# PSUM banks with two accumulators accessed in two rounds, the tail rows of the weight sums stored interleaved, and a new instruction order

## The chip, the core and the metric

The kernel runs on one core of a Trainium2 chip (TensorE, VectorE, ScalarE, GpSimd, the sync engine SP, and 16 DMA engines that all queues share). The metric is device time of one execution in microseconds. In the profile TensorE is PE (matmuls) and PEld (weight loads), VectorE is DVE, ScalarE is ACT and GpSimd is POOL.

## What is computed

Three blocks follow each other, each on the whole output of the one before. A recurrence over 768 tokens for 4x8 heads of width 40, a mixing block with two Fourier transforms and a channel MLP, and a mixing block with a token MLP and a channel MLP:

```python
for t in range(S):                                   # attention
    y[:, :, t] = einsum('bhd,bhde->bhe', rt, state)
    Sa = einsum('bhde,bhe->bhd', state, at)
    state = state * wt[:, :, None, :] - einsum('bhd,bhe->bhde', Sa, bt) + einsum('bhd,bhe->bhde', vt, kt)
...
u = x + real(fft(fft(x, axis=1), axis=2))            # block 1, x is 4 x 768 x 320
ch = relu(norm(u) @ w_ch1) @ w_ch2                   # 320 -> 1280 -> 320
x = u + ch
...
u = x + (relu(x.T @ w_tok1) @ w_tok2).T              # block 2, over tokens
out = u + relu(u @ w_ch1) @ w_ch2                    # 320 -> 1536 -> 320
```

The weights arrive as 64-bit floats; the kernel decodes them on the chip into a high and a low 32-bit part, and a product is three matmuls (high by high, high by low, low by high).

## The kernel before, in words

**Stages.** The recurrence runs in 12 chunks of 64 tokens. Then come block 1's channel MLP in six groups of 512 tokens, with the Fourier transforms of the next batch between them; the token MLP; and block 2's channel MLP, again in six groups. TensorE does all products, ScalarE and VectorE read PSUM (ScalarE makes the high part, VectorE subtracts it to get the low part), GpSimd adds.

**What sets the order.** The code makes a list of 4654 operations with costs and dependencies (class `Plan`). The string `ORDER`, found beforehand by a planner, says in which order they are written into the program; each engine then runs its own instructions in that order and none overtakes another. The keys that an operation reads and writes (lists `R` and `W` of `P.op`) are what the planner knows of its dependencies. The waits that are built into the program are not made from those keys: the tile framework makes them from the tiles, and takes a whole PSUM tile, here one bank, as one thing, in the order in which its accesses are written. A token `+m,bank,j` puts in m filler matmuls (`warm`, L54).

**The weight sums (`vset`).** Block 2's first channel weight is used in a scheme with seven products in place of eight (below), which needs sums of its quarters. While block 1's channel MLP runs on TensorE, VectorE and GpSimd decode four quarters, GpSimd forms the sums, and each of the seven matrices is split into a high part (tile `mdh`, three buffers, written by ScalarE at L838) and a low part, which go to a table `vS` in memory. There are four such sets: two column halves, each with 128-row parts (`part==0`, stored at L841) and with the 64 tail rows (`part==1`, stored at L842). A set makes 14 stores, on the SP queue:

```python
if part==0: ... nc.sync.dma_start(out=o(y),in_=fl(v()))
else: ... nc.sync.dma_start(out=o(2).rearrange("(a b p) n -> b a p n",a=2,b=2)[y],in_=fl(v())[0:64])
```

The tail's target has 2 blocks (a) of 32 rows (p) of 384 numbers; the source is 64 partitions. ScalarE can fill an `mdh` buffer again only when the store out of it has landed, and VectorE the buffers `mda`, `mdt` and `mdraw` likewise. Behind such a waiting instruction on ScalarE and VectorE stand the channel MLP's own instructions: `ch1` (L1049, tile `hps`, 8 matmuls of 512 columns) is followed by ACT L1051 and DVE L1052 (tile `cc`, high and low part), and `ch2` (L1039, tile `acc`, 12 matmuls of 320 columns) needs both.

**Another store for comparison.** `dr_T<-Y` (L992) has a target of 4 blocks of 32 rows: `s.Td[j][q].rearrange("p i x -> i p x")`, with i=4 first.

**The seven products (`ch7`, `ch1`).** A unit (36 of them: six groups by six) makes seven products of four matmuls of 256 columns (L1086), called 0 to 6 here. It has two banks, `sa` and `sb`, each with two accumulators of 256 columns: R0 and R1 in `sa`, R2 and R3 in `sb`. Product 0 goes to R0, 1 to R1, 2 to R2, 3 to R3; then 4 is added on to R0, 5 to R2 and 6 to R3. Between these the accumulators are read: ACT copies R0 (L1096) and R2 (L1099) after products 0 and 2, DVE adds R1 and R3 to earlier sums (L1093) after products 1 and 3. At the end R0 is read by the two relu steps (ACT L1091, DVE L1092), and R2 and R3 by DVE adds. Odd units use another pair of banks than even ones, so unit u+2 takes over the banks of unit u. `ch2` (L1075) is 12 matmuls of 320 columns into `acc`, twice a unit.

Of the kernel before, what the change touches and what calls it, by code (L numbers as in the profile page):

```python
# [540 lines left out]
34 85:1 32 35 86 36 83 37 88:1 38 8b:0 3a 89 8y 8e:1 8c 39 8f 3b 94 8k 3c 8l 93 3d 3e 92 3g 8m +7,y,0 95:0 3f 3h 9h:1 96 3i 9e:0 9i 3j 8o 3m 9b:1 9f
3n 8q 3k 98:0 9c 8p 3q ce:1 99 e6 8n e4 9k:1 cg kt 3l 8j cf 87 c1 84 8a 9l 3o 9p 9o 3p 3s c0 dx 8d e0 c2 9n e1 3t 8g e2 mv 97 3r 9g 3u 3x e5 hr 3v 3w
hx 9t e3 9q hs hw e7 ba ht e8 f3 e9 f2 hy b9 hu +12,y,0 ea:0 my bb 9r eb 9u bd 9v 9w +2,y,0 ej:1 ez 9x 9y 9z 9s a0 a1 bc a2 a3 +2,y,0 ed:0 fo a4 a5
be:2 qp ee a6 bf 48 bg a7 ek bh aa bi a8 +2,y,0 ep:0 em:1 a9 eq bj ab ca +3,y,0 bk:0 ae hp ac +1,y,0 bl bm af eg:0 ad bn eh ag f4:1 f5 ah en f6 aj bo
es +1,y,0 f7 ai el et bp mz ak 9a f9 +2,y,0 ck:2 al f8 an 9j am cl +2,y,0 ch:0 er ao cm ap cj ar ci 49 +2,y,0 cz:1 ev hv cs:1 d0 eu 4a cn:2 ct ef i0
fa:0 cv ey cu fb co cx:0 cw cq ew fc aq cy cp ex i1 d4:0 as cr f1 av fd d5 d1:1 f0 at 4b aw fe dc:0 fn az ff g1:1 d7 b0 dd d6 au hz g4:2 ax g3 9d d2
ib:0 g2 ay de ol g6 b3 i2:1 mw ic b1 g5 i8:0 i3 b4 ei df b2 ie:1 i9 id b5 b8 d9:0 i4 4c d3:0 4d d8 4e da 4i ga:0 if b7 eo db gb g7:1 4f b6 gc gn:1 4g
g9 4h ih:0 gp i5:1 k9 go k8 gi:2 4j ii 4k g8 k6 dg i6 4m gd:0 4n im ik gj ij di:0 il gl gk gq ge dl:1 ia gt:0 gg dm fp gr:1 9m fr dj i7 kb:1 dh dn fs
do gh +2,m,1 kc gu kd fq ke gm in gs gf +2,t,0 dk:0 ku 4l dp kf 4o kn:0 dq kg dr 4p dv ft:1 ko h6:0 ds fu ig kp:0 dt ec h7 fv:1 du kq gy:1 h8 fw ny h9
l8:2 gz ir ka is it iu ip gv:0 iv la iw l9 fx:0 k7 ix iy kr:1 h1 fy iz kv lb:0 gw ks j0 o2 j1 fz:0 ld tu h3:1 n0 lc kh:1 mx g0 ki io +1,y,0 kj h0 h4  # L550
n1 kk iq n2 o3:2 kl gx:0 j2 h2 km j3 h5 n6 j4 j5 ha n7 j7 lh:0 n8 hb hc:0 li hf:1 hd lj kw j6 hg +1,t,0 he:0 kx hh j8 hi le:1 kz jb hj lf j9 of:1 lg
on jc o4 og o5 vw jd o6 o0 oh:0 n3 o7 ly:1 jg o8 nc:0 ja oi lz hk oj:0 je n9:1 hl ok qr jf ky qq l0:1 jh lk:0 o1 n4 l1 hm lu:0 jk hn n5 m0:1 lp:1 4s
# [755 lines left out]
```

## Time and profile before

| | |
|---|---|
| median of 3 runs | 1048.67 us (1048.01 to 1056.04) |
| the profiled execution's own time | 1046.91 us |
| its span, first to last instruction | 1044.9 us |
| PE busy in the span | 942.1 us (90%) |
| DVE, ACT, POOL busy | 702.3, 492.2, 370.9 us |
| mean granted TensorE clock | 0.962 |

PE is the engine that is busy nearly always, but a busy PE is not a PE at its peak. So the stretches in which it is idle, or at a lower clock, and what ended each wait, are to be looked for. A mean over the whole span hides that the stages differ: some have almost no gap, two have many.

### The profile page before, as it was taken

How to read it: one execution, taken by the hardware profiler on the slowest of the kernel's cores; microseconds unless marked ns; L12 is line 12 of the kernel's file. 1: busy time of each engine (PE TensorE's matmuls, PEld its weight loads, DVE VectorE, ACT ScalarE, POOL GpSimd, SP SyncE). 2: the span in 40 equal slices, each digit the busy share in tenths (PEclk: the TensorE clock that was granted, in tenths of full speed). 3: DMA queues.
4: the chain of work that ended last, by engine and by line, in shares of the span. 5: the costliest groups of instructions: out<-in, count | busy, mean ns of one | idle time of the engine just before them, and what ended most of it. 6: DMA issues, size and time to landing. Idle time of an engine off the chain costs nothing.

```text
span 1044.9 us, 24118 instructions
## 1 busy us (share of the span) xinstructions
PE 942.1 (90%) x9621; PEld 857.4 (82%) x9621; DVE 702.3 (67%) x1543; ACT 492.2 (47%) x1068; POOL 370.9 (35%) x504
## 2 busy tenths in 40 slices
PE   7569999999999989999979869999998998998997
PEld 5558888888888888889858758999898888998887
DVE  8799598979687479996837235626767474654544
...
GB/s 219 182 153 144 188 192 192 180 206 193 174 161 204 269 273 249 210 150 101 127 88 160 41 88 89 127 334 219 153 86 83 64 41 41 85 47 21 1 33 25
DMA packets 153446, 146.13 MB, mean 140 GB/s; under 512 B 101303, under 2 KB 126967, under 8 KB 152567
## 3 DMA queue, kind: packets, MB, share of 16 engines
...
q14 instruction: 36, 0.29, 0.1%
...
## 4 chain that ended last, share of the span: by engine, by line
PE 32%; DVE 6%; DMA 6%; ACT 2%; POOL 2%; issue 2%; SPq 1%; DVEq 0%; ACTq 0%; POOLq 0%
PE acc L1075 10%; PE sb L1086 5%; PE hps L1049 5%; PE acc L1039 4%; PE sa L1086 4%; DMA dr_vS<-mdh 3%; PE tps L1182 2%; DVE W1t L1092 2%; DMA dr_vS<-mdraw 1%; DVE C L1093 1%; PE t2ps L1195 1%; DMA dr_vS<-mda 1%; DVE cc L1004 1%; ACT W1t L1091 1%; POOL C L1101 1%
## 5 line engine op out<-in xcount | busy, mean ns | idle before, releaser
L1039 PE MATMUL acc<-W,cc 128*128 128x320 f32 x720 | 123.4, 321 | 23.1 <-DVE cc L1052 17.2
L1039 PEld LDWEIGHTS acc<-W,cc 128*128 128x128 f32 x720 | 113.2, 195 | 31.2 <-DVE cc L1052 19.8
L1049 PE MATMUL hps<-cc,W1t 128*128 128x512 f32 x480 | 123.8, 403 | 1.0 <-DVE cc L1025 0.9
L1049 PEld LDWEIGHTS hps<-cc,W1t 128*128 128x128 f32 x480 | 90.4, 194 | 18.9 <-DVE cc L1025 1.4
L1101 POOL TENSOR_TENSOR C<-C,C 128x256 f32<-128x256 f32 x36 | 27.7, 770 | 209.4 <-DVE W1t L1092 105.8
L1093 DVE TENSOR_TENSOR C<-sb,C 128x256 f32<-128x256 f32 x108 | 44.9, 422 | 52.0 <-PE sb L1086 47.2
L1051 ACT ACTIVATE cc<-hps 128x512 fp32r<-128x512 f32 x60 | 35.5, 595 | 89.9 <-PE hps L1049 89.9
L54 PE MATMUL warm<-ident 128*128 128x128 f32 x450 | 74.2, 305 | 3.6 <-POOL ident masks.py:199 2.0
L1092 DVE SCALAR_TENSOR_TENSOR W1t<-C,W1t 128x256 fp32r<-128x256 f32 x108 | 46.1, 439 | 43.6 <-ACT W1t L1091 43.2
L1052 DVE SCALAR_TENSOR_TENSOR cc<-hps,cc 128x512 fp32r<-128x512 f32 x60 | 41.2, 687 | 50.2 <-ACT cc L1051 49.8
L226 POOL TENSOR_SCALAR_AFFINE_SELECT RT<-RT 64x384 f32<-64x384 f32 (+1 forms) x72 | 44.8, 643 | 78.3 <-ACT RT L136 73.9
L1075 PE MATMUL acc<-v,W1t 128*128 128x320 f32 x432 | 70.3, 314 | 2.4 <-DVE W1t L1092 1.0
L1091 ACT ACTIVATE W1t<-C 128x256 fp32r<-128x256 f32 x108 | 42.5, 414 | 63.3 <-DVE C L1093 60.5
L1075 PE MATMUL acc<-vb,W1t 128*128 128x320 f32 x432 | 68.7, 310 | 2.9 <-DVE W1t L1092 2.9
L216 PE MATMUL kg<-am,bt 120*128 120x192 f32 x242 | 55.8, 366 | 16.7 <-ACT am L136 13.2
L54 PEld LDWEIGHTS warm<-ident 128*128 128x128 f32 x450 | 65.1, 213 | 5.9 <-POOL ident masks.py:199 2.0
L417 POOL TENSOR_SCALAR_AFFINE_SELECT sc<-sc 64x384 f32<-64x384 f32 (+1 forms) x72 | 40.7, 565 | 80.9 <-ACT sc L136 78.8
L1075 PEld LDWEIGHTS acc<-v,W1t 128*128 128x128 f32 x432 | 65.1, 192 | 3.7 <-DVE W1t L1092 1.7
L1075 PEld LDWEIGHTS acc<-vb,W1t 128*128 128x128 f32 x432 | 63.7, 188 | 4.1 <-DVE W1t L1092 3.9
L216 PEld LDWEIGHTS kg<-am,bt 120*128 120x128 f32 x242 | 42.6, 208 | 21.8 <-ACT am L136 14.2
L407 PE MATMUL sc<-rm,VZd 120*128 120x192 f32 x264 | 58.7, 354 | 1.7 <-issue 1.1
L859 POOL TENSOR_TENSOR mda<-mda,mdh 128x320 f32<-128x320 f32 (+2 forms) x32 | 29.7, 934 | 82.9 <-ACT mdh L856 54.9
...
## 6 DMA issues: line engine op xcount, KB each, us to landing
...
```

The costliest lines, as they stand in the source:

```text
L54: for x in range(m): nc.tensor.matmul(t[:,128*(x%4):128*(x%4)+128],lhsT=ident,rhs=ident,start=True,stop=True)
L216: nc.tensor.matmul(ps[:,192*x:192*x+192],lhsT=bt[:,g+x].rearrange("p v t -> p (v t)"),rhs=am[:,:,g+x],start=True,stop=True)
L226: nc.gpsimd.affine_select(out=kv,in_=kv,pattern=[[0,3*m],[1,L]],compare_op=ALU.is_gt,fill=0.0,base=0,channel_multiplier=-1)
L407: for x,g in enumerate(gs): nc.tensor.matmul(ps[:,192*x:192*x+192],lhsT=VZd[:,g].rearrange("p v t -> p (v t)"),rhs=s.rm[:,:,g],start=True, ...
L1039: nc.tensor.matmul(s.pst(acc[x]),lhsT=a[:,sl],rhs=w2(w,m),start=(m==0 and n==0),stop=(m==MT-1 and n==2))
L1049: for n,(l,r) in enumerate(ops): nc.tensor.matmul(ps,lhsT=l,rhs=r,start=n==0,stop=n==7)
L1052: s.dve(.61,lambda: nc.vector.scalar_tensor_tensor(out=t["hl"][z],in0=s.pst(h),scalar=0.0,in1=t["hh"][z].bitcast(F32),op0=ALU.max,op1=ALU. ...
L1075: nc.tensor.matmul(s.pst(acc[x]),lhsT=a[:,sl],rhs=wv(w),start=(u==0 and y==0 and k==0),stop=(u==5 and y==1 and k==2))
L1086: for n,(y,x) in enumerate(((0,0),(0,1),(1,0),(2,2))): nc.tensor.matmul(R[r](),lhsT=va(q,y),rhs=S[:,x],start=first and n==0,stop=last and ...
L1091: s.act(256,lambda: nc.scalar.activation(out=Hh(y,c),in_=src(),func=AF.Relu),rd,[('Hh',z,y,c)],free=free)
L1092: s.dve(.33,lambda: V.scalar_tensor_tensor(out=Hl(y,c),in0=src(),scalar=0.0,in1=Hh(y,c).bitcast(F32),op0=ALU.max,op1=ALU.subtract),rd+[('H ...
L1093: def add(n,r,m,free): s.dve(.33,lambda: V.tensor_tensor(out=C(n),in0=R[r](),in1=C(m),op=ALU.add),[K[r],('C',m)],[('C',n)],free=free)
```

## The change

Four things are changed. The keys of the accumulators become the banks themselves: the planner now takes two accumulators of a bank as one thing. The code of a unit is written so that accesses to a bank alternate in two rounds: both first products, both reads, the later product or products, the last reads. The tail rows' target is walked with p first and a second, and the host lays out the weight's tail rows so that each comes twice in a row (row 2p+a is tail row p for both a), which leaves the contents of `vS` as they were. The estimate of that store's cost is .00097 for .00095 per column. `ORDER` is a new string for all 4654 operations, with 235 filler matmuls where there were 225.

```diff
 ORDER="""
-0 1 5 4 7 8 2 6 3 9 1e 1g 1i a 3y 1h 7q 1f 40 41 e 44 42 3z f g 43 45 b c h 7o +12,y,0 c3:0 fm j bx c4 i bq:1 8t k c5:0 br l m bs:1 1j o n 46 1k d 47
+0 1 5 4 7 8 2 6 9 3 1e 1g a 1i 3y 1h 1f 7q 40 41 44 e 42 3z f g 43 45 b c j h 7o +12,y,0 c3:0 fm i bq:1 c4 bx k c5:0 8t l br m 1j bs:1 o n 46 1k d 47
...
@@ vset
-                else: P.op('SP',.5,lambda y=y,v=v,o=o: nc.sync.dma_start(out=o(2).rearrange("(a b p) n -> b a p n",a=2,b=2)[y],in_=fl(v())[0:64]),kv,[('mv',c,q,2+y)],due=due,data=d*.00095)
+                else: P.op('SP',.5,lambda y=y,v=v,o=o: nc.sync.dma_start(out=o(2).rearrange("(a b p) n -> b p a n",a=2,b=2)[y],in_=fl(v())[0:64]),kv,[('mv',c,q,2+y)],due=due,data=d*.00097)
@@ ch7, ch1
-            K=[pa+(0,),pa+(1,),pb+(0,),pb+(1,)]
+            K=[pa,pa,pb,pb]
...
-            x0=prod(0,0,True,False,[ha[0],hb[0]])
-            s.act(256,lambda: nc.scalar.activation(out=C(p1),in_=R[0](),func=AF.Copy),[K[0]],[('C',p1)],free=fa)
-            prod(1,1,False,True,after=[x0]); add(u2,1,p1,fa)
-            x2=prod(2,2,True,False,after=[x0])
-            s.act(256,lambda: nc.scalar.activation(out=C(p5),in_=R[2](),func=AF.Copy),[K[2]],[('C',p5)],free=fb)
-            prod(3,3,False,False,after=[x2]); add(u3,3,u2,fb)
+            x0=prod(0,0,True,False,[ha[0],hb[0]]); prod(1,1,False,True)
+            s.act(256,lambda: nc.scalar.activation(out=C(p1),in_=R[0](),func=AF.Copy),[K[0]],[('C',p1)],free=fa); add(u2,1,p1,fa)
+            prod(2,2,True,False,after=[x0]); prod(3,3,False,False)
+            s.act(256,lambda: nc.scalar.activation(out=C(p5),in_=R[2](),func=AF.Copy),[K[2]],[('C',p5)],free=fb); add(u3,3,u2,fb)
...
-            prod(5,2,False,True); add(c12,2,u2,fb); relu(0,1,lambda: C(c12),[('C',c12)])
-            prod(6,3,False,True); add(c21,3,u2,fb); relu(1,0,lambda: C(c21),[('C',c21)])
+            prod(5,2,False,True); prod(6,3,False,True)
+            add(c12,2,u2,fb); relu(0,1,lambda: C(c12),[('C',c12)])
+            add(c21,3,u2,fb); relu(1,0,lambda: C(c21),[('C',c21)])
@@ kernel (host layout)
-            f = [np.arange(128), 128 + np.arange(128), np.tile(np.arange(256, 288), 4), np.tile(np.arange(288, 320), 4)]
+            f = [np.arange(128), 128 + np.arange(128), np.tile(np.repeat(np.arange(256, 288), 2), 2), np.tile(np.repeat(np.arange(288, 320), 2), 2)]
```

**Place 1, SP queue, the last set of tail stores (second column half).** Before (L842 is the tail store, L825 and L852 are loads of weights; the numbers behind the shape name the semaphores waited for):

```order
L825 DMA mdraw0_4881<-in_moe2_w_ch1_dram 128x768 [waits DMAHW4_49]
L842 DMA dr_vS_183<-mdh0_4884 2x32x384 [waits DMAHW5_49,Activation_49]
L842 DMA dr_vS_183<-mdh0_4884 2x32x384 [waits Activation_49]
L842 DMA dr_vS_183<-mdh1_4888 2x32x384 [waits DMAHW7_49]
L842 DMA dr_vS_183<-mdt1_4886 2x32x384 [waits DMAHW0_49,Pool_49]
```

And now (the tail store is L843, the loads L826 and L853):

```order
L842 DMA dr_vS_183<-mdh1_4888 128x384 [waits DMAHW4_49]
L843 DMA dr_vS_183<-mdh1_4888 32x2x384 [waits Activation_49]
L843 DMA dr_vS_183<-mdh0_4884 32x2x384 [waits DMAHW6_49,Activation_49]
L843 DMA dr_vS_183<-mda2_4891 32x2x384 [waits DMAHW7_49,Pool_49]
L843 DMA dr_vS_183<-mdh0_4884 32x2x384 [waits DMAHW0_49,Activation_49]
```

The stores stay 14 a set, in another sequence; their target's first dimension is 32 where it was 2.

**Place 2, PE in the first group of the seven-product stage, just behind the second block of `acc` matmuls.** Before, two units alternate (banks `sa_8889` and `sb_8894` are one unit's, `sb_8820` the unit before it):

```order
L1086 MATMUL sa_8889<-cc_5535,vc_8273 128x256 [waits DMASW3_49]
L1086 MATMUL sa_8889<-cc_5535,vc_8273 128x256 x3
L1086 MATMUL sb_8894<-cc_5535,vc_8273 128x256 [waits DMASW2_49,DVE_49]
L1086 MATMUL sb_8894<-cc_5535,vc_8273 128x256 x3
L1086 MATMUL sa_8889<-cc_5535,vc_8273 128x256 x4
L1086 MATMUL sb_8894<-cc_5535,vc_8273 128x256 x4
L1086 MATMUL sb_8820<-cc_5535,va_8138 128x256 [waits DVE_49]
L1086 MATMUL sb_8820<-cc_5535,va_8138 128x256 x3
L1086 MATMUL sb_8820<-cc_5535,va_8138 128x256 [waits Activation_49]
L1086 MATMUL sb_8820<-cc_5535,va_8138 128x256 x3
```

And now (`sa_8900` and `sb_8915` are one unit's, `sa_8828` and `sb_8833` the unit before it):

```order
L1087 MATMUL sa_8900<-cc_5555,vc_8286 128x256 [waits DMASW3_49,DVE_49]
L1087 MATMUL sa_8900<-cc_5555,vc_8286 128x256 x7
L1087 MATMUL sa_8828<-cc_5555,va_8190 128x256 [waits DVE_49,Activation_49]
L1087 MATMUL sa_8828<-cc_5555,va_8190 128x256 x3
L1087 MATMUL sb_8915<-cc_5555,vc_8286 128x256 [waits DMASW2_49]
L1087 MATMUL sb_8915<-cc_5555,vc_8286 128x256 x3
L1087 MATMUL sb_8833<-cc_5555,va_8190 128x256 [waits DVE_49,Activation_49]
L1087 MATMUL sb_8833<-cc_5555,va_8190 128x256 x7
L1087 MATMUL sb_8915<-cc_5555,vc_8286 128x256 x4
```

Products 0 and 1 stand together (x1 and x7), and 5 and 6 of the earlier unit stand together behind one wait, where they were two steps with a wait each.

**Place 3, DVE in the second group.** Before, the two last reads of bank `sb_9143` stand apart (C is a sum, L1092 the low part of a relu, L988 and L989 transposes for a later group):

```order
L1093 TENSOR_TENSOR C5_8741<-sb_9143,C1_8737 128x256 [waits DVE_49,PE_49]
L1092 SCALAR_TENSOR_TENSOR W1t_5548<-sa_9134,W1t_5548 128x256 [waits Activation_49]
L989 STREAM_TRANSPOSE Y_5534<-X_4867 128x4x32 [waits DMAHW6_49,DMAHW7_49,DMAHW5_49,DMAHW4_49]
L988 STREAM_TRANSPOSE Y_5534<-X_4867 128x2x4x32
L989 STREAM_TRANSPOSE Y_5534<-X_4867 128x4x32 x3
L988 STREAM_TRANSPOSE Y_5534<-X_4867 128x2x4x32 x2
L989 STREAM_TRANSPOSE Y_5534<-X_4867 128x4x32 x2
L1093 TENSOR_TENSOR C4_8740<-sb_9143,C1_8737 128x256
L1092 SCALAR_TENSOR_TENSOR W1t_5548<-C4_8740,W1t_5548 128x256 [waits Activation_49]
L1093 TENSOR_TENSOR C1_8737<-sa_9217,C0_8736 128x256 [waits PE_49]
```

And now (the adds are L1094, the low part L1093):

```order
L1094 TENSOR_TENSOR C5_8747<-sb_9154,C1_8743 128x256 [waits DVE_49,PE_49]
L1094 TENSOR_TENSOR C4_8746<-sb_9154,C1_8743 128x256 [waits DVE_49]
L1094 TENSOR_TENSOR C1_8743<-sa_9228,C0_8742 128x256 [waits DVE_49,Activation_49]
L1094 TENSOR_TENSOR C3_8745<-sb_9237,C1_8743 128x256 [waits DVE_49,Activation_49]
L1093 SCALAR_TENSOR_TENSOR W1t_5568<-C4_8746,W1t_5568 128x256 [waits Activation_49]
```

Both last reads of a bank stand together, and so do the next unit's two adds.

## Rows read from the trace of the kernel before

**Rows 1.** The page's first line.

```profile
span 1044.9 us, 24118 instructions
```

**Rows 2.** Busy time by stretch: us; busy (instructions) of PE, PEld, DVE, ACT, POOL; PEclk, DMA share, GB/s.

```profile
520.00:625.00 105.00, 81.83 (x402) 70.87 (x401) 46.95 (x110) 29.02 (x64) 36.82 (x37) 0.89 0.29 95
625.00:703.00 78.00, 78.00 (x445) 70.45 (x444) 38.14 (x74) 22.78 (x45) 29.09 (x37) 1.00 0.59 173
758.00:1045.00 287.00, 258.54 (x1834) 246.08 (x1834) 162.09 (x422) 92.78 (x269) 57.53 (x76) 0.99 0.14 47
```

**Rows 3.** Waits, 500 to 625 us: total us, times, longest.

```profile
ACT mdh L838 <- DMA dr_vS<-mdh: 26.4, 8, 7.1
PE acc L1039 <- DVE cc L1052: 16.4, 6, 8.7
...
DVE mda L855 <- DMA dr_vS<-mda: 9.5, 2, 7.6
...
PE acc L1039 <- ACT cc L1051: 5.8, 4, 3.7
```

**Rows 4.** DVE's timeline, 600 to 620 us: start, us, instruction, idle before it.

```profile
610.48 0.49 DVE L855 SCALAR_TENSOR_TENSOR mda<-mdraw,mdt 128x320 int32<-128x320 int32 x1 [7.56 <-DMA dr_vS<-mda]
...
611.50 0.68 DVE L1052 SCALAR_TENSOR_TENSOR cc<-hps,cc 128x512 fp32r<-128x512 f32 x1
```

**Rows 5.** Busy time by stretch: tail stores alone, `dr_T` stores alone, 128-row stores.

```profile
602.00:611.00 9.00, 1.51 (x8) 1.03 (x6) 1.37 (x4) 0.47 (x1) 0.00 (x0) 0.77 0.13 50
865.00:869.00 4.00, 3.26 (x25) 2.84 (x23) 0.17 (x1) 0.97 (x3) 0.00 (x0) 1.00 0.26 102
...
497.00:499.00 2.00, 2.00 (x15) 1.81 (x15) 1.93 (x4) 1.09 (x2) 1.47 (x2) 1.00 1.02 368
```

**Rows 6.** The chain that ended last, 584 to 618 us: start, us, what.

```profile
579.89 4.27 DMA dr_vS<-mdh
...
587.33 10.44 DMA dr_vS<-mdh
...
601.35 10.96 DMA dr_vS<-mdraw
```

**Rows 7.** PE's timeline, 505 to 640 us.

```profile
527.29 1.73 PE L1039 MATMUL acc<-W,cc 128*128 128x320 f32 x10 [1.49 <-DVE cc L1052]
528.86 2.02 PE L1049 MATMUL hps<-cc,W1t 128*128 128x512 f32 x8
...
535.95 3.04 PE L1039 MATMUL acc<-W,cc 128*128 128x320 f32 x10 [4.23 <-DVE cc L1052]
...
612.24 3.04 PE L1039 MATMUL acc<-W,cc 128*128 128x320 f32 x10 [8.72 <-DVE cc L1052]
...
622.73 2.56 PE L1049 MATMUL hps<-cc,W1t 128*128 128x512 f32 x8
```

**Rows 8.** Waits of the weight loads, 757 to 1045 us: total us, times, longest.

```profile
PEld sb L1086 <- ACT C L1099: 9.2, 16, 1.5
PEld sb L1086 <- DVE C L1093: 7.9, 9, 1.6
PEld sa L1086 <- ACT C L1096: 7.6, 12, 1.4
PEld acc L1075 <- DVE W1t L1092: 5.7, 7, 1.6
PEld sb L1086 <- DVE W1t L1092: 3.1, 4, 1.6
```

**Rows 9.** The chain, 760 to 766 us.

```profile
762.00 1.43 PE sb L1086 x12
763.43 1.76 PE acc L1075 x12
```

**Rows 10.** Groups by shape, 700 to 1045 us: busy us, mean ns, idle before and releasers.

```profile
L1093 DVE TENSOR_TENSOR C<-sa,C 128x256 f32<-128x256 f32 x36 | 15.2, 423 | 13.3 <-PE sa L1086 7.3 <-ACT W1t L1091 2.3 <-issue 2.2
...
L1096 ACT ACTIVATE C<-sa 128x256 f32<-128x256 f32 x36 | 13.7, 381 | 67.1 <-PE sa L1086 57.8 <-DVE C L1093 6.2 <-issue 2.9
```

More of the change, by code (lines that the diff above doesn't have):

```diff
@@ L541 @@
[L541 to L552, printed above, removed]
@@ new lines @@
+1mj +6,t,0 1lw:0 1mp 1m1 1mk 1mr 1mh 1mx:0 1mt 1ms 1oq 1m2 1n6 1ov 1oy 245 1mw:2 1mv:1 1p8 246 1oz 1p9 1p0 1mu 1n7 1p5 1pb +10,t,0 1n2 247 1my 1n8 248
+1n9 1n3 24d 1mz 1p1 1m3 1ot 1n4 1qb 1n0 1n5 1qi 1na +10,t,0 1nf:2 1qd 24a 1n1 1ng 249 +1,y,0 1nb:0 1pc 24g 1nh 1ou 1q1 1nc 1ni 24i 1nd 1qf 24e 1ow 1pi
+24b 1ne 24j 1pa 1qc +7,acc,0 22z:0 299 234:1 24f 24c 1pd 232 230 235 1pe 231 +2,acc,0 239:0 237 1qe 233 1p2 1pg 23d:1 1pf 236 1pr 238 24o:0 1pj 1qk
+23c 250:1 1qh 1q2 23a 1pl 23b 24h 23e 298 23f 1pm 23g 1qn 1q3 23h 251 29g 24p 1p3 23i 252 23j 253 24q 1p4 254 24r +12,acc,0 24k:1 23k 1qg 1p6 23l
@@ new lines @@
+25v 1rl 1rk 1s2 25t 1rp 1rn 264 1rm 1s3 25w:1 1sb 1rs 1s4 1ro 25u 1rt 1rq 1rv 1ru 1s9 25z 29m 25x 1rz 1rw 1s5 1sl 1rx 276:0 1sc 1s6 1ry 1sv 1sd 1s0
+277 1s7 25y 1se 1sf +2,ps,0 26a:1 1sm 1sg 1s8 278 279 1sn 1sa 1sj 1sh 26d 1t5 26b 265:0 1sp 1sw 1sq 27a:1 1si 266 268 267 1sx 1sk 26e:0 27b 1sz 269
+1t6 27c 29r:1 26c 29n:0 26f 1sy 1t7 27d 26g 1t0 29o 1so 26h 1t9 26i 29s 1st 1sr 29p 27e 1t8 26j 26k 1td 29q 1tb 26l 1tr 26m 1tf 2a3:0 26n 1t1 29t 26o
+29u 26v 27h 26t 1ta 26x:1 2cp 1tl 29v:1 26y 26w 26u 270:0 1tc 26z 29w 271 29x +1,acc,3 273:1 1t2 27f 1te 29y 274 272 +2,acc,3 29z:1 1ss 1t4 275 1t3
@@ new lines @@
+27i 1su +1,acc,1 27j:0 27g 2co 28h 1tg 2cq 27m:1 27k 1th 27l 1tm 27p:3102 1ti 27n 2cr 28k 1tn 2cs 2cx 27o 27q:0 1ts 28j 1tt 2cy 27t 27r 1tj 2cz 1to
+1u0 28e 1tp 27u:1 1tu 1tq 27s 28f 27x 2ct 27v 2cu 28i 1tv 28g 28l 2a4 27y:0 2d0 2cv 1tw 2a5 27w 1tk 1u7 281 2a0 1u9 27z 1u1 1vb 1tx 2a1 280 282:1 1tz
+1ty 28m:0 285 1u8 28n 1uf 28o 1ua 283 1u2 1ub 286:0 1uj 1ud 1u3 284 1uk 1uh 2a2 1ul 28p:1 1u4 1um 287 289 28q 1u5 1uz 288 1u6 28a:0 2cw 1ug 28r 28d
+1uc 1ui 1ur 28b 1us 1ue 1un 28c 28v:1 1uo 1uu 1vc 1uq 1vd 28y 1up 28w 2a6 1ve 1v5 1uv 1vf 28z:0 1v0 1uw 28x 2a7 1v1 1uy 28s:1 290 1v2 292 28t 1v3 291
@@ new lines @@
+22o 2it 2iu 2iz 2j0:1 2ix 2iy 2j3 2j4:0 2j1 2j2 2j7 22w 22y 2f6 2fe 2fl 2fj 2fg 2fi 2f7 2fc 2f9 2fh 2f8 2fa 2ff 2fb 2fd 2fk 2j5 2jd 2jn 2jl 2jj 2jp
+2je 2jm 2jr 2jt 2j6 2j8 2jk 2jo 2jv:1 2jz:0 2ju 2jq 2js 2jw 2k0 2jf 2jg 2ji 2jh 2jc 2jb 2k7 2k8 2k3 2k4 2k5 2k6 2jx 2jy 2kf:1 2k1 2k2 2kr:0 2ks
++2,acc,1 2kp:0 2kd 2ke 2k9 2ka 2kb 2kc 2kg 2kh 2l6 2l5 2kq 2kt:0 2l4 2l2 2l3 2l7 2ki 2ku 2la 2l8 2l9 2kn:1 2ko 2kz 2l1 2l0 2lc 2le 2ld 2ja 2kj:0 2md
+2me 2mh 2kk 2kl 2mi 2mn 2mo 2j9 2km 2kx:1 2ky 2kv:0 2kw 2ml 2n1:1 2n2 2n5:0 2n6 2mj 2mk 2n3:1 2n4 2mf 2mg 2mp:0 2mt:1 2mm 2mq 2mu 2nb 2nc 2nd 2ne 2mr
```

219 lines of the change are left out of this document (108 added, 111 removed).

## The prediction

> **What bounds the kernel now.** I read the profile in this order: the page's head, the busy time by stretch, the waits of the stretches with gaps, and then the timelines and the chain at the longest waits.
>
> The span is 1044.9 us [rows 1]; the profiled execution took 1046.91 us, so 2.0 us lie around the span, and it stands 1.8 us under the median of 1048.67. The sum below is made against 1044.9 + 2.0. By stretch [rows 2], PE has two kinds of life. From 625 to 703 us it is busy 78.00 of 78.00 us at granted clock 1.00; nothing can be won there. From 520 to 625 it is busy 81.83 of 105 at clock 0.89, so 23.2 us are idle and some of the busy time is slow. From 758 to 1045 it is busy 258.54 of 287 at clock 0.99, so 28.5 us are idle in many small pieces (at the weight loads, which come just ahead of the matmuls, a little more is idle). The change touches just these two stretches. In both, DVE, ACT and POOL are busy less than 57% [rows 2]: they don't lack time, they wait in line.
>
> *500 to 625.* PE waits 16.4 us in 6 waits for DVE's `cc`, and 5.8 in 4 for ACT's, 22.2 in all, while ACT waits 26.4 us for stores out of `mdh` to land, and DVE 9.5 out of `mda` [rows 3]. The link is the in-order queue: at 610.48 DVE's L855 has sat 7.56 us on a store out of `mda`, and the `cc` instruction that PE wants starts only behind it, at 611.50 [rows 4]. PE's `acc` row at 612.24 then shows 8.72 us of idle ended by that `cc` [rows 7]. Why do the stores land late? While tail stores run alone, the DMA share is 0.13 and 50 GB/s flow: two engines' worth of sixteen. A transfer with 4 as its target's first dimension has 0.26 and 102 GB/s, and the 128-row stores of the same set 1.02 and 368 GB/s [rows 5]. A tail store is 2x32x384x4 B = 98,304 B, so 1.97 us at 50 GB/s; one that finds nothing ahead lands in 4.27 us, those behind others in 10.44 and 10.96 [rows 6]. Then the clock: after the idle times seven of PE's rows are slow, from the one at 535.95 (3.04 us, where the same `acc` row takes 1.73) to the one at 622.73 (2.56 against 2.02) [rows 7]. A 3.04 us row is one largely at 1.2 GHz in place of 2.4. The seven excesses sum to 8.4 us. This stretch so loses 22.2 + 8.4 = 30.6 us.
>
> *758 to 1045.* The weight loads wait for reads of the banks `sa` and `sb` by ACT's copies and DVE's adds: 9.2 + 7.9 + 7.6 = 24.7 us in 37 waits of at most 1.6 us; the next two, 5.7 and 3.1 us, are for the low part of relu, that is for a reader at a unit's end [rows 8].
>
> **The change part by part.**
>
> *Tail stores.* They stay 28 of 96 KB, their target becomes 32x2x384. The bytes are the same. Rows show 2 first for two engines, 4 first for four, 128 first for all [rows 5]; 32 first is not among them. Nearest to 32 are the two ends 4 and 128: between 102 and 368 GB/s, a store takes between 0.96 and 0.27 us, and 28 of them 27 or 7.5 us where 55 are spent now. I take the 128 end, because the share doubled when the first dimension did, and 32 gives each of 16 engines two rows. The Trainium skill ("DMA: Bandwidth & Descriptors", section "Why a DMA increments its semaphore by 16 and not by 1") has a rule: the number of engines is the largest one up to 16 that divides the slowest dimension of both sides. By it the old store had 2 engines, which agrees with 0.13 [rows 5], and the new one has 16; that it is 16 for 32 no run here shows yet. By the rule the part gains the 26 us worked out below; by the row with 4 it gains some 15.
>
> What is won: with landings near the fixed part (4.27 - 1.97 = 2.3 us, plus 0.3 to 1.0) rather than 10 us, three `mdh` buffers are enough for ACT, and the 22.2 us of PE's idle time and the 8.4 us of slow clock that follows it have no cause left. What is late next is the chain of a set itself: load, DVE, POOL's sums, ACT's high part, DVE's low part, store. Its engines are busy 46.95, 29.02 and 36.82 of 105 us [rows 2], so it fits beside some 24 us of PE work per set, but not without a wait where ACT refills a buffer whose store has just gone. I leave 1.15 us for each of four sets, 4.6 in all. **Gain 26 us**, at most 30.6. At the least 15: if the four-engine price held and half of the waits stayed (11.1) with half of the slow clock (4.2). On the SP queue stores and loads only change places (14 stores a set before and now); a load behind a store's wait is issued earlier when that wait is shorter. The host's doubled tail rows are no work on the chip.
>
> *Two rounds per bank.* The waits that are built in take a bank as one thing, in the order of the writing. Before, product 1 went to R1 beside R0, and the add of R1 or a later product stood behind accesses that it has no need of: in the written order 20 of the 36 adds of R1 stand behind product 4, though only R0 is touched by that. What decides whether PE waits is the distance from a write to the next write of the same bank, counted in PE's own work: a product is 1.43/3 = 0.48 us, an `acc` row 1.76 [rows 9]. Counted so through the order of before, product 1 to 4 is 2.0 us on average, 13 of 36 under 1.2; product 3 to 5 is 3.1; 5 to 6 is 3.1 with six under 1. Through the order of now: 1 to 4 is 6.0 (least 1.8), 3 to 5 is 6.4 (one of 0.5, the next 2.2), and 5 and 6 stand together. Between the writes one ACT copy (0.381 us) and one DVE add (0.423) [rows 10] have to be done, 0.8 us back to back; with what lies between them I put 1.3, an estimate from the longest waits of 1.4 to 1.6 [rows 8]. Before, many distances were shorter than that or were so with one other instruction ahead in the reader's queue; now only one is. So nearly all of the 24.7 us lose their cause: I take 22.
>
> What it costs: a bank is held longer. The next unit but one gets `sa` 5.2 us after the last write (9.2 before), `sb` after 4.5 (4.8); 34 handovers each. Before, `sb` at 4.8 cost 3.1 us in 4 waits [rows 8]; `sa` at 5.2 should then cost nearly the same, and I take 2 us more than now. The stage's products and `acc` rows are the same 252 of the one and 72 of the other. **Gain 20 us**; at least 8 (a third of the 24.7 goes, as it would if the queues of ACT and DVE and not the distances made the waits), at most 28 (all 24.7, and 3.1 of the handover).
>
> A rule of the skill speaks against this part: "Perfetto Trace Analysis", section "Matmuls", has independent matmul groups rotate through different PSUM banks, so that reading one overlaps the next one's matmuls; putting two products into a bank before either is read is the contrary. What it would do here is rival (d).
>
> *The rest of the order.* The recurrence moves by neighbouring swaps, less than one place on average; its instructions are the same. Ten more fillers stand where PE waits anyway. I take nothing for it, and 5 us either way.
>
> Sum: 1044.9 - 26 - 20 = 998.9, with 2.0 around the span **1001 us**.
>
> **Rivals.**
>
> (a) *Bank waits only move.* ACT and DVE read the same accumulators in their queues' order, and the idle time before PE goes to handovers, to `acc` waiting for relu's low part (5.7 us now, [rows 8]), or to the readers' queues. Then the stores alone gain: 1047 - 26 = 1021 (1014 to 1028). For it: in the stage DVE is busiest beside PE, 162.09 of 287 [rows 2], and waits of others came to 8.8 us already. Against it: 162 leaves room.
>
> (b) *The set's chain becomes the bound* and gives back half of the store gain: 1047 - 13 - 20 = 1014. For it: DVE, POOL, ACT and the queue pass a quarter on in turn, and each wait blocks others. Against it: the busy shares [rows 2].
>
> (c) *Stores stay slow, or something else in the set is the bound* (the change doesn't do what it says there): 1047 - 20 = 1027 (1020 to 1036). For it: no row has first dimension 32. Against it: 2, 4 and 128 all scale.
>
> (d) *Slower: the banks' handover.* With two products in a bank in each round, and both reads behind both writes, the next unit's product 0 could wait for POOL's and DVE's late sums in each unit. 34 handovers of two banks; to cancel the 46 us they must wait 1.35 us each unit on both banks together, and at 1.7 us (the longest waits of now are 1.6, [rows 8]) they cost 58 us: 1047 - 46 + 58 = 1059. Against it: `sb` has had such a distance all along, with 3.1 us in 4 waits.
>
> (e) *Nothing*: the new order sets up as many waits as it takes away: 1047.
>
> **How the numbers follow.** The forecast, both parts working (988 to 1013), 0.57; (a) 0.15; (b) 0.10; (c) 0.09; (d) 0.05; (e) 0.04. The low end is all of both gains with the order's 5 us: 1047 - 30.6 - 28 - 5 = 983, say 984; the high end takes in (a) and half of (c), 1027. Below it less than 0.05 is left out, above some 0.13. About 1% is what a measurement of this kernel can tell from no change, so faster by that means under 1038: the forecast, (a), (b) and nearly all of (c), less a little, 0.88; within 1% 0.07; slower 0.05.
>
> **What the changed profile would show.** Stores: while tail stores run alone, a DMA share near 1 (at 0.13 or 0.26 that step is wrong) and landings under 6 us; ACT's wait for stores out of `mdh` under 8 us; PE's waits for `cc` under 6 and its clock from 520 to 625 at 0.97 or more. If the clock recovers but the waits stay, (b) is it. Banks: the three waits for the copies and the adds together under 5 us; the waits for relu's low part no more than 11. If those or new ones at the handover take the place of the 24.7, (a) or (d) is it. The forecast is wrong most likely where the distance, counted on PE alone, doesn't see that a reader stands behind others in its own queue.

## The result and the profile after

The changed kernel takes 970.04 us (median of 4 runs, 967.6 to 973.94), the kernel before 1049.83 (median of 4 as well): a ratio of 0.9234, interval 0.9182 to 0.9286. The forecast was 1001 us, in a range from 984 to 1027. The direction was right, the gain of 80 us is far over the 46 forecast, and it lies outside the range.

The page of the changed kernel, its first line and the busy times (engine, us, share, instructions), against [rows 1]:

```profile
span 965.9 us, 24197 instructions
...
PE 910.0 (94%) x9641; PEld 842.3 (87%) x9641; DVE 712.1 (74%) x1543; ACT 492.1 (51%) x1068; POOL 374.8 (39%) x504
```

Where the time went is seen by cutting both traces at the same places of the program: the first `hps` matmul (start of block 1's channel MLP), the first `tps` (token MLP), the last `t2ps` (from there on the stage of the seven products), the end. First the kernel before, then the changed one; columns as in [rows 2].

```profile
415.20:703.80 288.60, 262.01 (x1431) 232.31 (x1431) 173.97 (x378) 95.31 (x211) 117.99 (x128) 0.95 0.44 136
703.80:752.40 48.60, 46.08 (x303) 43.76 (x302) 33.40 (x81) 14.62 (x37) 17.95 (x21) 1.00 0.56 176
752.40:1044.90 292.50, 263.61 (x1875) 250.74 (x1873) 165.44 (x433) 93.55 (x271) 59.72 (x80) 0.99 0.16 53
```

```profile
417.10:669.10 252.00, 249.65 (x1438) 224.58 (x1437) 178.37 (x376) 93.97 (x209) 119.50 (x127) 1.00 0.52 157
669.10:715.80 46.70, 46.08 (x310) 44.66 (x309) 32.20 (x81) 14.69 (x37) 17.45 (x21) 1.00 0.53 170
715.80:965.90 250.10, 246.32 (x1867) 245.12 (x1865) 165.49 (x434) 94.34 (x271) 59.15 (x80) 1.00 0.19 63
```

Block 1 lost 36.6 us, the token MLP 1.9, the seven-product stage 42.4; all that comes ahead took 1.9 more. In both large parts PE is now busy nearly throughout, at clock 1.00. Of the waits of [rows 3] this is left between 417 and 669 us:

```profile
ACT mdh L839 <- DMA dr_vS<-mdh: 4.4, 2, 2.6
...
DVE mda L856 <- DMA dr_vS<-mda: 0.6, 1, 0.6
```

PE's waits for `cc` in `acc` rows are gone (0.3 us at their weight loads remain), and of the 37.6 us that the weight loads of before waited from the last `t2ps` on (the view's rows summed; most are in [rows 8]) about one is left:

```profile
PEld sb L1087 <- DVE C L1094: 0.4, 1, 0.4
PEld sa L1087 <- DVE C L1094: 0.4, 2, 0.2
PEld acc L1076 <- DVE W1t L1093: 0.3, 1, 0.3
```

And while tail stores run all but alone the DMA share is 0.73, where it was 0.13 [rows 5]; 0.73 of sixteen is nearly twelve engines' work (a window of the changed kernel, 1.5 us):

```profile
581.00:582.50 1.50, 1.50 (x9) 1.23 (x8) 0.92 (x2) 0.10 (x2) 0.67 (x1) 1.00 0.73 184
```

### The profile page after: what moved, and what is told of

The parts are those of the page before. It is cut to its first block, busy times and chain, and to the rows that moved or that the text cites. A ratio compares the mean times of both kernels' runs of the same rounds, so it can differ in the third digit from the quotient of the medians.

```text
span 965.9 us, 24197 instructions
## 1 busy us (share of the span) xinstructions
PE 910.0 (94%) x9641; PEld 842.3 (87%) x9641; DVE 712.1 (74%) x1543; ACT 492.1 (51%) x1068; POOL 374.8 (39%) x504
## 5 line engine op out<-in xcount | busy, mean ns | idle before, releaser
L1050 PE MATMUL hps<-cc,W1t 128*128 128x512 f32 x480 | 121.0, 396 | 0.9 <-DVE cc L1053 0.8
L1040 PE MATMUL acc<-W,cc 128*128 128x320 f32 x720 | 116.0, 310 | 0.0
L1040 PEld LDWEIGHTS acc<-W,cc 128*128 128x128 f32 x720 | 109.2, 188 | 4.7 <-ACT mdh L839 0.3
L1050 PEld LDWEIGHTS hps<-cc,W1t 128*128 128x128 f32 x480 | 87.8, 188 | 17.8 <-DVE cc L1053 1.1
L1094 DVE TENSOR_TENSOR C<-sb,C 128x256 f32<-128x256 f32 x108 | 44.2, 420 | 33.4 <-PE sb L1087 27.0
L1076 PE MATMUL acc<-v,W1t 128*128 128x320 f32 x432 | 67.4, 309 | 0.0
L1092 ACT ACTIVATE W1t<-C 128x256 fp32r<-128x256 f32 x108 | 42.0, 413 | 45.5 <-DVE C L1094 36.6
L1093 DVE SCALAR_TENSOR_TENSOR W1t<-C,W1t 128x256 fp32r<-128x256 f32 x108 | 46.6, 449 | 19.5 <-ACT W1t L1092 19.1
L407 PE MATMUL sc<-rm,VZd 120*128 120x192 f32 x264 | 56.7, 344 | 1.4 <-ACT sc L136 0.7
```

The lines of the kernel that those rows point to most:

```text
L407: for x,g in enumerate(gs): nc.tensor.matmul(ps[:,192*x:192*x+192],lhsT=VZd[:,g].rearrange("p v t -> p (v t)"),rhs=s.rm[:,:,g],start=True, ...
L1040: nc.tensor.matmul(s.pst(acc[x]),lhsT=a[:,sl],rhs=w2(w,m),start=(m==0 and n==0),stop=(m==MT-1 and n==2))
L1050: for n,(l,r) in enumerate(ops): nc.tensor.matmul(ps,lhsT=l,rhs=r,start=n==0,stop=n==7)
L1076: nc.tensor.matmul(s.pst(acc[x]),lhsT=a[:,sl],rhs=wv(w),start=(u==0 and y==0 and k==0),stop=(u==5 and y==1 and k==2))
L1092: s.act(256,lambda: nc.scalar.activation(out=Hh(y,c),in_=src(),func=AF.Relu),rd,[('Hh',z,y,c)],free=free)
L1093: s.dve(.33,lambda: V.scalar_tensor_tensor(out=Hl(y,c),in0=src(),scalar=0.0,in1=Hh(y,c).bitcast(F32),op0=ALU.max,op1=ALU.subtract),rd+[('H ...
```

## The experiments

Every experiment is the kernel before with one edit in the stores, or with another order of the same 4654 operations, or both, so their line numbers are one or two lower (products L1085, adds L1092, copies L1095 and L1098, relu L1090 and L1091). "Stage" is the time from the last `t2ps` to the end, "block 1" that from the first `hps` to the first `tps`, both of the profiled run. These lengths are compared rather than whole times, because what comes ahead of block 1 took between 414 and 425 us in these runs, with the same operations. Each length is from one profile. How far the stage varies by itself is seen where its order is the same: 292.5, 294.3 and 296.8 us with the order of before, 250.1, 250.2 and 249.9 with the new one.

### One part alone: stores, order, and the order of each stage

The first has the new store and layout with the order of before, the second the new order with the old store:

```diff
-... o(2).rearrange("(a b p) n -> b a p n",a=2,b=2)[y] ...      np.tile(np.arange(256, 288), 4)
+... o(2).rearrange("(a b p) n -> b p a n",a=2,b=2)[y] ...      np.tile(np.repeat(np.arange(256, 288), 2), 2)
```

> The order of before, word for word, and only the tail rows of the weight sums stored interleaved. If the two-engine stores are the whole cause of the gap in block 1 (theory), block 1 takes 33 to 37 us less than before, the seven-product stage keeps its 292 us, and the time is about 1012 us. If the order sought anew did a part of it (rival), this kernel gains only the 26 us forecast or less, about 1022 us, with waits for cc left in 500 to 625 us.

Measured: 1020.28 us, ratio 0.9693 (0.9645 to 0.9741). Block 1 and the stage of this kernel:

```profile
424.20:678.80 254.60, 250.92 (x1430) 225.37 (x1431) 175.78 (x378) 95.61 (x211) 118.72 (x128) 0.99 0.50 154
...
727.50:1021.80 294.30, 265.46 (x1875) 252.24 (x1873) 165.47 (x433) 93.56 (x271) 59.85 (x80) 0.99 0.16 53
```

Block 1 is 34.0 us shorter, as the theory had it, and the stage does not gain. The time is 8 us over the 1012 expected; in the profiled run, what comes ahead of block 1 took 9.0 us more than in that of before. PE's idle time in block 1 went from 26.6 us (288.6 - 262.0) to 3.7, its busy time from 262.0 to 250.9 with as many matmuls, at a granted clock of 0.99 where it was 0.95: 22.9 us of waiting and 11.1 us of slow clock.

> The order of the changed kernel, with the tail stores and the layout of the weight rows as before. Theory: block 1 keeps its whole gap (36 us over the changed kernel) and the seven-product stage takes the 250 us of the changed kernel: about 1005 us. Rival (the order has moved stores or loads so that the slow stores hurt less): 985 to 995 us, with less than half of the 26 us that ScalarE waited for stores out of mdh.

Measured: 1003.09 us, 0.9544 (0.9501 to 0.9588). Block 1 takes 282.3 us, 30.3 more than in the changed kernel where 36 were expected; most of ScalarE's and VectorE's waits for the old stores are there:

```profile
ACT mdh L837 <- DMA dr_vS<-mdh: 23.7, 4, 9.9
DVE mda L854 <- DMA dr_vS<-mda: 13.7, 2, 10.0
...
PE acc L1038 <- DVE cc L1051: 9.9, 3, 7.9
```

So the new order alone doesn't mend the stores: the 23.7 us are not under half of before's 26.4, as the rival wanted. The stage has the 250.2 us of the changed kernel.

The next two join one order's first part to the other's last, both with the new stores: `ORDER` = new up to the first product, then old; and old up to the last part of the token MLP, then new.

> Interleaved stores; the new order up to the first product of the seven-product stage, from there on the order of before. Theory: the two parts add, the stage has the 292 us and the same-bank waits of before (24 us), time 1010 to 1014 us. Rival (the stage of before was slow because of what came ahead of it, late loads or transposes): the stage falls under 280 us, time under 1000.

> Interleaved stores; the order of before up to the last part of the token MLP, from there on the new order. Theory: as fast as the changed kernel, 968 to 973 us, since in block 1 the stores alone make the gain and in the stage the new order alone. Rival (the new order makes a part of block 1's gain): 978 us or more, the loss being in block 1.

Measured: 1019.39 us, 0.9718 (0.9655 to 0.9781), stage 296.8, both some 5 us over what was expected; and 970.59 us, 0.9242 (0.9205 to 0.928), stage 249.9, as expected, with the keys and the code of a unit as in the kernel before: what counts of the new keys is the order that came of them. The stage is as fast as its own order makes it, whatever ran ahead of it, and the new order ahead of it is worth 3.5 us of block 1 (254.6 against 251.1). So the stores are worth 30 us in the time by themselves (1050.3 to 1020.3), the order of the stage alone 50 more (1020.3 to 970.6; 44 in the stage itself), and the whole new order 47 with the old stores (1050.3 to 1003.1): the two parts add.

### Two rounds, and nothing else

What do the two rounds change? Not that two products are written ahead of the first read of their bank: in the program text of before, too, products 0 and 1, and 2 and 3, stand ahead of it in all 36 units. New is that product 4 stands behind the add of R1 (ahead of it in all 36 units before) and product 5 behind the add of R3 (ahead of it in 31), with 6 mostly right behind 5. In TensorE's own sequence 0 and 1 are neighbours in 11 units before and in 13 now, 5 and 6 in 5 and in 33.

Here the order of before was changed by moves of at most eleven places only, with ScalarE's and VectorE's sequences nearly as they were (14 of 1042 and at most 20 of 1515 instructions stand up to nine places elsewhere). In the first of the three, reads and writes of each bank alternate as in the changed kernel in all 72 cases. TensorE in units 15 and 16 (P0.15 is product 0 of unit 15; the first line is the order of before), first all banks, then `sa` alone, then only product 4 behind the add of R1:

```diff
-P0.15 P2.15 P3.15 P1.15 P4.15 P5.15 P0.16 P2.16 P3.16 P1.16 P6.15 P4.16 P5.16 P6.16
+P0.15 P1.15 P2.15 P3.15 P0.16 P1.16 P2.16 P3.16 P4.15 P5.15 P6.15 P4.16 P5.16 P6.16
+P0.15 P1.15 P2.15 P3.15 P5.15 P0.16 P1.16 P2.16 P3.16 P4.15 P6.15 P5.16 P4.16 P6.16
+P0.15 P2.15 P3.15 P1.15 P5.15 P0.16 P2.16 P3.16 P1.16 P4.15 P6.15 P5.16 P4.16 P6.16
```

> Interleaved stores and the order of before, in which each unit's operations are only moved by a few places so that its banks are accessed in two rounds (products 0 and 1 together, both reads, 4; products 2 and 3 together, both reads, 5 and 6 together). Counted on PE the distance from 1 to 4 is then 6.6 us and from 3 to 5 it is 6.5, as in the changed kernel; everything else stands as in before. Theory (two rounds are what the gain comes from): the stage takes 250 to 258 us, all waits for the copies, the adds and relu's low part under 6 us in sum, time 975 to 985. Rival 1 (the forecast: only the same-bank waits go, the other 12.7 us stay): stage about 268 to 272. Rival 2 (the order sought anew is what does it): stage over 280.

Measured: 1021.97 us, 0.9739 (0.9675 to 0.9803), as slow as with the stores alone; the stage takes 301.2 us. Its row and its waits:

```profile
720.80:1022.00 301.20, 266.25 (x1879) 258.45 (x1877) 166.03 (x433) 94.09 (x271) 59.27 (x80) 0.95 0.16 52
```

```profile
PEld acc L1074 <- DVE W1t L1091: 10.8, 11, 2.4
PEld acc L1074 <- ACT W1t L1090: 9.1, 5, 4.1
PEld sa L1085 <- DVE W1t L1091: 7.4, 5, 2.3
PEld sb L1085 <- DVE C L1092: 5.8, 5, 2.3
PEld sb L1085 <- ACT C L1098: 2.0, 1, 2.0
```

The three same-bank waits fell from 24.7 us to 7.8, and the waits for relu's results grew from 10.9 (5.7, 3.1, 1.2 and 0.9 in before) to 28.7, with 1.4 for `sb` that stand further down; part of them are at the handover of `sa`. In sum the weight loads wait 38.9 us here and 37.8 with the stores alone. The mean granted clock of the stage is 0.95, and 0.83 from 880 to 920 us. So the theory and the first rival are out, the second rival's "over 280" holds, and the prediction's rival (a), "bank waits only move", is what two rounds alone do. One place shows why. TensorE, then ScalarE, then VectorE:

```profile
992.09 0.64 PE L1085 MATMUL sa<-cc,vc 128*128 128x256 f32 x4
992.57 1.93 PE L1074 MATMUL acc<-v,W1t 128*128 128x320 f32 x12
994.34 1.11 PE L1085 MATMUL sb<-cc,W1t 128*128 128x256 f32 x8
999.34 1.17 PE L1074 MATMUL acc<-v,W1t 128*128 128x320 f32 x3 [3.89 <-ACT W1t L1090]
```

```profile
995.94 0.42 ACT L1090 ACTIVATE W1t<-C 128x256 fp32r<-128x256 f32 x1 [5.75 <-DVE C L1092]
996.26 0.37 ACT L1095 ACTIVATE C<-sa 128x256 f32<-128x256 f32 x1
996.53 0.41 ACT L1090 ACTIVATE W1t<-C 128x256 fp32r<-128x256 f32 x1
998.29 0.38 ACT L1098 ACTIVATE C<-sb 128x256 f32<-128x256 f32 x1 [1.36 <-POOL C L1100]
998.57 0.71 ACT L1090 ACTIVATE W1t<-C 128x256 fp32r<-128x256 f32 x2
999.18 0.37 ACT L1090 ACTIVATE W1t<-sa 128x256 fp32r<-128x256 f32 x1
```

```profile
995.48 0.42 DVE L1092 TENSOR_TENSOR C<-sb,C 128x256 f32<-128x256 f32 x1 [4.50 <-PE sb L1085]
```

The `acc` row at 999.34 is unit 32's and needs that unit's last relu, the second of the two at 998.57. Ahead of it in ScalarE's queue stand, from 995.94 on, a relu of unit 33 (which waits for VectorE's add at 995.48, and that for product 5 at 994.34) and a copy of unit 34 that waits 1.36 us for GpSimd. The relu at 999.18 reads what product 4 had left in `sa` at 992.09: over six microseconds in line, and as long a hold on the bank.

> The same, but for bank sa alone: products 0 and 1 together, both reads, then 4; bank sb as before (distance 3 to 5 is 2.9 us, 5 and 6 apart). Theory: the waits of sa (7.6 + 1.2 us) go and those of sb (9.2 + 7.9) stay, stage 276 to 284, time 1000 to 1010. Rival (waits only move: sb's grow by what sa's lose): stage within 3 us of the 294 of the kernel with stores alone.

> Interleaved stores and the order of before, in which only product 4 is put behind the add of R1 where it stood ahead of it: the distance from 1 to 4 becomes 6.0 us, products 0 and 1 stay apart. Theory (the distance decides, not that two products stand together): within 4 us of the kernel with bank sa in two rounds. Rival (products standing together is what helps, one wait less): within 3 us of the kernel with stores alone, and slower than the one with sa in two rounds by 8 us or more.

Measured: 1024.27 us, 0.9747 (0.9683 to 0.9811), stage 301.1; and 1032.77 us, 0.9837 (0.9765 to 0.991), stage 312.5 (in the longest of its four runs, 1040.07 us). With `sa` alone in two rounds its waits for the copies are gone and those of `sb` grew from 17.2 to 24.6 us (15.2 and 9.4); the second, with a distance of 6.0 us from product 1 to 4, is the slowest of all with new stores, at a stage clock of 0.94. In both kernels theory and rival missed the stage's length: a longer distance on TensorE gained nothing, by either way.

### The wait on the whole bank, without another sequence

> Interleaved stores and the new order, every engine with the same sequence as in the changed kernel, but written so that ScalarE's copy of R0 (R2) comes between products 0 and 1 (2 and 3) in the program in 39 of 72 places, so that the second product has to wait for the copy of the other half of its bank. Theory (the waits are made from whole banks in the order of writing): 39 new waits of PE for ACT of 0.6 to 1.0 us each, stage 25 to 40 us longer than the changed kernel, time 995 to 1010. Rival (a wait for the other half costs nothing, PE has other work in its queue): within 5 us of the changed kernel.

```diff
 program text, a unit of the new order (each engine's own sequence stays)
-P0  P1  copy R0  ...  P2  P3  copy R2
+P0  copy R0  P1  ...  P2  copy R2  P3
```

Measured: 1010.59 us, 0.9624 (0.9566 to 0.9683); the stage takes 289.7 us, 39.6 more than the 250.1 of the changed kernel, at the expectation's upper end (the time as well). Two rows appear that it doesn't have:

```profile
PEld sb L1085 <- ACT C L1098: 22.4, 17, 2.6
PEld sa L1085 <- ACT C L1095: 9.7, 12, 2.1
```

So the waits are made from whole banks in the order of writing, and such a place costs 39.6/39 = 1.0 us on average, with what the clock lost (0.98 in the mean of the stage, 1.00 in the changed kernel). As views show them the waits are less: PE's own idle rows for these two sum to 25.8 us only.

### The readers' queues

Three TensorE sequences (two rounds by local moves, before, new), with the 14 reads of each unit on ScalarE and VectorE in the order in which their inputs become ready. ScalarE in units 15 and 16 with two rounds (cpR0 is the copy of R0, H00 the relu of R0, H01, H10 and H11 the relus of the sums; transposes left out):

```diff
-cpR0.15 cpR2.15 cpR0.16 cpR2.16 H11.15 H10.15 H01.15 H01.16 H00.15 H10.16 H00.16 H11.16
+cpR0.15 cpR2.15 cpR0.16 H00.15 cpR2.16 H11.15 H01.15 H10.15 H00.16 H11.16 H01.16 H10.16
```

H00.15, one of the two last reads of `sa`, stood behind a relu of the next unit.

> TensorE's sequence as in the kernel with two rounds by local moves (stage 301 us), but the 14 reads of each unit on ScalarE and VectorE put into the order in which their inputs become ready, counted along TensorE's sequence. Theory (a wait depends on what a read stands behind in its own queue, not on the distance of the writes): the waits of acc for relu and of sa for the handover, 17 and 7 us there, go, stage 252 to 270 us, time 975 to 993. Rival (distance and rounds are all that counts, or the rest of the new order is needed): stage 290 or more.

> TensorE's sequence as in before, products of a bank apart, with interleaved stores; only the reads on ScalarE and VectorE sorted in the same way. If the readers' order alone is the cause: stage 255 to 270 us. If both are needed (theory): the waits for copies and adds of the same bank stay near the 25 us of before, stage 275 to 290.

> TensorE's sequence as in the changed kernel, the reads sorted in the same simple way in place of the order sought anew. Theory: nothing about the sought order of the readers is special beyond standing in the order of readiness, stage 250 to 262 us, time within 10 us of the changed kernel. Rival (the search found more than that): stage over 265.

Measured: 989.97 us (0.9443, 0.9368 to 0.9518), 994.75 (0.9482, 0.9405 to 0.9559) and 989.94 (0.9414, 0.9331 to 0.9498); stages of 264.4, 271.4 and 265.3 us. The first is the cleanest pair of all: TensorE's sequence and the order of reads and writes at every bank are those of the kernel with two rounds by local moves, only what stands ahead of a read in ScalarE's and VectorE's queues differs, and the stage is 36.8 us shorter (301.2 to 264.4), as the theory had it:

```profile
718.70:983.10 264.40, 252.00 (x1879) 248.82 (x1877) 161.93 (x433) 99.00 (x271) 59.66 (x80) 0.99 0.18 59
```

The middle one is the surprise, and lies between its two ranges: with TensorE's sequence as before, 23 of the 44 us are gone, and of the same-bank waits 5.7 us are left instead of the "near 25" expected:

```profile
PEld sa L1085 <- ACT C L1095: 3.4, 7, 1.8
...
PEld sb L1085 <- ACT C L1098: 1.7, 4, 0.8
...
PEld sb L1085 <- DVE C L1092: 0.6, 2, 0.3
```

That too speaks for readers that stood in line. But this pair is less clean: sorting also wrote the copy of R0 ahead of product 1 in 24 units and that of R2 ahead of product 3 in 8, so that the copy need not wait for the second product, and the second product has to wait for the copy. What that was worth was not measured by itself. The third, 0.3 us over its rival's 265, says that readiness alone is not yet the sought order: 15 us are missing.

A second rule puts all reads of the stage first, and transposes and other work for later groups (T) only where no read is ready within 0.4 us. From here on all that comes ahead of the last part of the token MLP is in the new order. VectorE with TensorE's new sequence, from unit 10 to 11 (L: relu's low part), sorted, reads first, and with later transposes:

```diff
-+R1.10 +R3.10 T L11.10 L00.10 T T T +c12.10 +c21.10 T +R1.11 L01.10 L10.10 +R3.11 L11.11 T T L00.11
++R1.10 +R3.10 L11.10 L00.10 T T T T +c12.10 +c21.10 +R1.11 L01.10 +R3.11 L10.10 T T T L11.11 T T L00.11
++R1.10 +R3.10 L11.10 L00.10 T T T T T +c12.10 +c21.10 +R1.11 L01.10 +R3.11 L10.10 T T T T L11.11 T T T L00.11
```

> Interleaved stores, the new order up to the last part of the token MLP; then TensorE's sequence of before (products of a bank apart), with all reads of the stage (copies, adds, relu, final adds) on ScalarE and VectorE in order of readiness, and the transposes for later groups only where no read is ready within 0.4 us. If the readers' queues are all that costs (theory now): stage 251 to 259 us, time within 1% of the changed kernel. If the two rounds are worth something of their own (rival): stage over 263, with waits for the copies left.

> The same with TensorE's sequence of the two rounds by local moves. Theory: 251 to 259 us as with the sequence of before. Rival: faster than that by 6 us or more.

> The same with TensorE's sequence of the changed kernel; stage 265 with reads sorted by readiness alone, 250 in the changed kernel. Theory (what is left there are transposes and final adds ahead of reads): 251 to 259 us. Rival (the sought order does something else, too): over 262.

Measured: 1003.22 us (0.956, 0.9502 to 0.9618), 991.31 (0.9431, 0.9386 to 0.9476), 987.18 (0.9396, 0.9352 to 0.944); stages 278.2, 266.9, 267.7. All three missed the 251 to 259 us, for a cause of my own making: the rule wrote transposes into VectorE's queue ahead of the landing of a store, and all reads behind them stood too (VectorE waits 20.2, 16.9 and 21.6 us for such stores). VectorE of the third:

```profile
796.84 0.45 DVE L987 STREAM_TRANSPOSE Y<-X 128x256 f32<-128x256 f32 x1 [9.78 <-DMA dr_T<-Y]
```

The last three write them later, where the stores would have landed at the plan's 2.9 us each, one behind the other (and 0.2 us in place of 0.4):

> TensorE's sequence of before, reads first as in the last three, but the transposes of VectorE are written only where the stores ahead of them would have landed (2.9 us a store, one behind the other), so that VectorE does not stand 4 to 10 us on a store with reads behind it. Theory (readers' queues are all): the waits of 5 to 7 us go, stage 254 to 262 us. Rival (rounds are worth something of their own): stage 266 or more, and 8 us or more over the two with rounds.

> The same with the two rounds by local moves. Theory: within 6 us of the one with the sequence of before. Rival: 8 us or more less than it.

> The same with TensorE's sequence of the changed kernel. Theory: 252 to 260 us in the stage; what is still missing to the 250 of the changed kernel are a few waits of over 1 us that can be named. Rival: over 264, so that the sought order does something that readiness does not describe.

Measured: 989.6 us (0.9442, 0.9379 to 0.9504), 982.31 (0.9377, 0.9327 to 0.9428), 978.59 (0.9341, 0.9292 to 0.9389). Stage rows of the three kernels, in this order:

```profile
717.30:985.70 268.40, 254.66 (x1875) 250.41 (x1873) 172.90 (x433) 101.95 (x271) 61.52 (x80) 0.99 0.18 58
```

```profile
716.70:977.20 260.50, 252.01 (x1879) 248.94 (x1877) 170.21 (x433) 101.37 (x271) 60.52 (x80) 0.99 0.18 60
```

```profile
717.40:974.30 256.90, 248.89 (x1866) 247.74 (x1865) 169.66 (x434) 101.68 (x271) 60.73 (x80) 0.99 0.18 61
```

All the stages of these runs, with interleaved stores:

| TensorE's sequence | readers of before | sorted | reads first | late transposes | as sought |
|---|---|---|---|---|---|
| before | 294.3 | 271.4 | 278.2 | 268.4 | not run |
| two rounds, local moves | 301.2 | 264.4 | 266.9 | 260.5 | not run |
| new | not run | 265.3 | 267.7 | 256.9 | 249.9 |

Read along the second row: at the same TensorE sequence and the same order at the banks, the readers are worth 36.8 us, and 40.7 with late transposes. Read down the columns: with two rounds the stage is shorter by 7.0, 11.3 and 7.9 us once the readers are sorted (4.8, 11.9 and 7.3 in the times), where it is longer by 6.9 with the readers of before (1.7 in the time). Part of the 7 to 11 us can be the 32 places named above, at which a copy stands between two products of its bank; the first row has them in all three sorted kernels, the other rows have none. TensorE's own new sequence counts little: 265.3 against 264.4, and 256.9 against 260.5. The theory "readers are all" so falls short by 7.9 us, nearly the 8 that its rival asked for; of the 256.9 in the last row, 4.7 us are two waits that can be named (3.0 for VectorE's last step of the token MLP, 1.7 for a low part, `cc` L1006), the rest of the 7 us to the sought order is spread. None of these beats the changed kernel.

## Why the prediction was wrong

**Tail stores: right in kind, 4 to 8 us short in size.** The target with 32 first uses the engines that 2 first left idle (0.73 against 0.13), and the four-engine end of my range is out. The rule of the Trainium skill that the prediction weighed ("DMA: Bandwidth & Descriptors", "Why a DMA increments its semaphore by 16 and not by 1") agrees with this. Forecast 26 us, at most 30.6; measured 34.0 in block 1 with the old order, 30.3 with the new one, 30 in the time. Of the terms, 22.2 us of idle time were 22.9; the slow clock was 11.1, not the 8.4 of the seven rows I had picked; and the 4.6 us that I kept back for ScalarE's refills cost TensorE nothing: ScalarE still waits 4.4 us, beside other work. Rivals (b) and (c) are out by the first two runs.

**Two rounds per bank: wrong in size and in mechanism.** The step that failed is "what decides whether PE waits is the distance from a write to the next write of the same bank, counted in PE's own work", and the 22 us drawn from it. The kernel with two rounds by local moves has distances as long as the changed one's (6.6 and 6.5 us against 6.0 and 6.4) and the same order of reads and writes at every bank, and is no faster than the stores alone: stage 301.2. What decides in the main is what the read in between stands behind in ScalarE's and VectorE's queues: with these two put in order and TensorE's sequence left alone, the stage falls to 264.4. A read that is ready can stand six microseconds behind another unit's, and a longer distance on TensorE only makes other reads the late ones. The forecast's last sentence named this danger, but gave it no price. The prediction's picture of the change was off, too: product 4 was ahead of the add of R1 in all 36 units, not in 20, and that products 0 and 1 stand together, as the lines of Place 2 show it, is no rule of the new order (13 units).

**The size of the stage's gain.** I took the 24.7 us of same-bank waits as what could be won and left the other 12.7 us of the weight loads' waits standing, with 28 as the most for all. But the stage's own work was there to be multiplied out: 252 products at 1.43/3 and 72 `acc` rows at 1.76 [rows 9] are 120.1 + 126.7 = 246.8 us, and the stage took 292.5. So 46 us were lost, and 42.4 were won. The rows of waits show less because TensorE's idle time there is 28.9 us (292.5 - 263.6) and the other 17.3 are in its "busy" time: with the same products it is busy 246.3 us now. A small part of that is slow clock (the granted clock was 1.00 up to 1000 us and 0.95 behind); the rest I take to be waits so short that the modelled end of one matmul covers them, which no row shows.

**The handover** cost nothing in the changed kernel, against the 2 us that I took. Rival (d) is out there; but it has a core, for with two rounds and the old readers `sa` waits 7.4 us for relu's low part, where the kernel with stores alone has 1.1. The rule of the Trainium skill that the prediction set against this part ("Perfetto Trace Analysis", "Matmuls": independent matmul groups rotate through different banks) is not put to the test by this pair, since the order of before, too, writes two products into a bank ahead of its first read.

**The rest of the order** I priced at nothing, 5 us either way: block 1 gained 2.6 to 3.5, the token MLP 1.9, and the part ahead moved by less than it moves from run to run.

The span forecast, 998.9 us, was 33.0 over the 965.9 measured: 22.4 from the stage, 10.6 from block 1, 1.9 from the token MLP, less 1.9 for the part ahead. What isn't settled: why the search found readers in so much better an order this time. That its keys now say what the program waits for is a likely cause, but only argued; a new search with the old keys was not tried. A tail store on four engines was not run either. Nor was TensorE's sequence of before with sorted readers and no copy between two products of a bank, which would tell the price of the rounds by itself.
